# Last 64 rows of three weight matrices on partitions 0 to 63, in 8-row transfers, used as K=64 matmuls

## The chip, the cores and the metric

One core of one Trainium2 chip runs the whole kernel. The metric is the device time of one execution in microseconds (us), the median over the runs.

## The reference

A decode step for one token: attention with a K/V cache of 8 heads x 65,536 positions x 256 (bfloat16), a gated feed-forward block, and a scalar gate between the two. Cut to what matters:

```python
x: [1, 1, 448]                    # D = 448 = 3 * 128 + 64
q    = x @ wq                     # wq [448, 4096], 16 query heads of 256
a    = softmax(q k^T / 16) v @ wo # k_cache, v_cache: 268 MB each
gate = x @ W_gate;  up = x @ W_up # [448, 1792] each
b    = (gate * (gate > 0) * up) @ W_down
out  = g * a + (1 - g) * b        # g = sigmoid(sum(x * gate_w))
```

Almost all bytes are the cache. The change touches only `wq`, `W_gate` and `W_up`, and of those only the last 64 of 448 rows (the *remainder*), which do not fill 128 partitions.

## The kernel before

Three SBUF buffers of 8 MB form a ring. The cache is streamed in 8 MB tiles (32 for K, 31 for V, and a last V tile in pieces), all issued by one queue (SP). `ring[2]` first holds `wq`, `W_gate`, `W_up` and then `W_down`. So the *third K tile* can only be issued when the matmuls of `W_down` are done.

```python
order = [("wq", 0, 8.7), ("k", 0, TILE), ("gu", 0, 7.7), ("wd", 0, 3.8)]   # then k1, k2, k3, v0, k4, ...
slot, held, freed = {}, {2: ["gu", "dn"]}, {}     # ring[2] is free after gate/up and W_down
# ...
# remainder: 64 rows cut in two halves, 128 partitions, row r in partitions 2r and 2r+1
l_["wqh"] = dma("sp", ..., wqh, A_wq[NR3:D, :].rearrange("r (t n) -> (r t) n", t=2))
dma("sp", ..., wfh[i_], W[NR3:D, :].rearrange("r (t f) -> (r t) f", t=2))
# ...
def f_gu(e):                                      # gate/up, 28 output columns of M_ps
    for ft in range(FT):
        for which in range(2):
            c = which * 14 + ft
            for kt in range(R3):                  # three matmuls with K=128
                e.matmul(GU_ps[:, c:c + 1], wf3[which][:, kt * F + ft:(kt + 1) * F:FT], xT[:, kt:kt + 1],
                         start=(kt == 0), stop=False, skip_group_check=True)
            for half in range(2):                 # two matmuls, 64 output partitions each
                ins = e.matmul(GU_ps[64 * half:64 * half + 64, c:c + 1], wfh[which][:, ft:F // 2:FT],
                               xT[:, R3 + half:R3 + half + 1], start=False, stop=True, skip_group_check=True)
# ... cut: score, softmax, P x V, output projection
```

The program of PE (the matmul engine; DVE below is the vector engine) runs in this order at the start: q (with `wq`), gate/up, the scores of the first K tile, `W_down`.

## Time and profile before

| | before |
|---|---|
| time, median of 3 runs | 1287.91 us (1287.82 to 1288.36) |
| time of the profiled execution, one more | 1287.13 us |
| bytes loaded | 549 MB, 428 GB/s over the span |
| DMA, PE, DVE | 99% of 16 DMA engines, 33%, 49% |
| steady distance of two tiles | 19.36 us |

The execution that the profile shows was 0.7 us faster than the fastest of the timed ones.

The page of the kernel before, cut to its span, the busy times of the compute engines (us, share, x instructions) and two DMA queues (packets, MB, share of 16 engines):

```profile
span 1285.3 us, 9821 instructions
...
PE 430.0 (33%) x4554; PEld 161.6 (13%) x4554; DVE 633.8 (49%) x421; ACT 61.4 (5%) x115; POOL 4.1 (0%) x21
...
q1 hardware_dynamic: 12754, 549.03, 99.1%
q8 instruction: 35, 0.57, 0.2%
```

The load queue q1 keeps the 16 DMA engines busy for practically the whole span; no compute engine comes near. The second queue, q8, loads instructions: 35 packets.

The DMA issues of the kernel before (what is loaded, the issuing queue, count, KB each, us from issue to landing):

```profile
ring<-in_A_wq_dram SPq DMA_DIRECT2D x1, 3072.0 KB, 10.1
...
ring<-in_A_wq_dram SPq DMA_DIRECT2D x1, 512.0 KB, 10.9
ring<-in_A_k_cache_dram SPq DMA_DIRECT2D x32, 51.6
ring<-in_A_v_cache_dram SPq DMA_DIRECT2D x31, 36.7
...
ring<-in_B_W_up_dram SPq DMA_DIRECT2D x1, 224.0 KB, 35.2
```

A tile needs 19.36 us of transfer but lands 37 to 52 us after its issue: two or more tiles are always queued. An engine that finishes its part of one tile goes on with the next at once (within some 4 ns in the median, from the packet records). There is one place at the start where this is not so. The timeline of the kernel before, 36 to 66 us (start, duration, engine, line, operation):

```profile
39.34 0.31 PE L418 MATMUL M_ps<-xT,ring 128*128 128x1 bf16 x3 [16.49 <-DMA ring<-in_B_W_up_dram]
39.58 0.28 PE L421 MATMUL M_ps<-xT,ring 128*64 128x1 bf16 x2
39.79 0.34 PE L418 MATMUL M_ps<-xT,ring 128*128 128x1 bf16 x3
...
52.79 5.05 PE L345 MATMUL ST<-ring,xm 128*16 128x512 bf16 x64
57.64 2.81 PE L434 MATMUL A_ps<-ring,hT 128*1 128x448 bf16 x14
60.48 0.80 SPq L442 DMA_DIRECT2D ring<-in_A_k_cache_dram  x2
```

Gate/up starts when `W_up` has landed and repeats a group of three and two matmuls every 0.48 us, up to 52.8 us; the first scores and `W_down` follow; at 60.48 the queue issues the next two K tiles. That the queue really waited for `W_down` is told by the waits of the issuing queue (who waited for whom: total us, times, longest):

```profile
SPq L507 <- PE ST L345: 951.9, 30, 36.5
...
SPq L442 <- PE A_ps L434: 37.6, 1, 37.6
```

The first line is an ordinary wait for a ring buffer with a full queue behind it. The second is the one that matters. In the packet records of the trace the second K tile runs out on the 16 engines between 61.0 and 62.8 us, 0.5 to 2.3 us after that issue, and the median engine then needs 20.94 us for the third K tile instead of 19.35: about 1.6 us lost. I call this the *restart loss*.

Transfer times count here from the first instruction of each trace, as the timelines do. The prediction counts its transfer times from another zero, 0.24 us earlier in this trace: its "61.2 to 63.0" is the 61.0 to 62.8 above.

Last, where the end comes from. These are the 16 landings (each 0.3 to 0.5 us after the end of a packet, so taken as one per DMA engine; sorted, us after the first) of one transfer each in the trace of the kernel before:

```
second K tile     first 61.43   0 .08 .12 .15 .16 .18 .32 .33 .46 .52 .53 .58 .74 1.49 1.76 1.78
third K tile      first 82.28   spread up to 2.52
last whole V tile first 1243.42 0 .17 .26 .35 .37 .49 .84 | 4.14 6.11 6.19 6.20 6.28 6.38 6.44 | 8.38 8.61
```

The engines drift apart over the run. Seven stay together, one ends 4 us behind, six about 6 us, two 8.4 to 8.6 us behind. The last one sets the end: in 15 of the 18 traces of this case the execution ends 34.7 to 35.5 us after that last landing.

### The profile page before, as it was taken

The numbers are of one execution on the slowest core, as the hardware profiler recorded it, in microseconds if no ns is written. First come the engines' busy times: TensorE is split into PE (matmuls) and PEld (weight loads), VectorE is DVE, ScalarE is ACT, GpSimd is POOL, SyncE is SP. The second block draws the span as 40 slices with busy tenths as digits, with TensorE's granted clock in tenths as the row PEclk, the third lists the DMA queues.
The fourth block names the chain that finished last, engine by engine and source line by source line (L and its number), as shares of the span: only waits on it lengthen the run. The fifth ranks groups of instructions, "written<-read, shape, count | busy, mean of one in ns | idle before, by whom it ended". The sixth has DMA issues, their size and how long they took to land.

```text
span 1285.3 us, 9821 instructions
## 1 busy us (share of the span) xinstructions
PE 430.0 (33%) x4554; PEld 161.6 (13%) x4554; DVE 633.8 (49%) x421; ACT 61.4 (5%) x115; POOL 4.1 (0%) x21
## 2 busy tenths in 40 slices
PE   3624322334123432224331333331323323233236
PEld 2401110111001110001110111110101101011111
DVE  2588633465433655434555443555434556335600
ACT  0000000000000000000000000000000000000000
POOL 1000000000000000000000000000000000000000
PEclk8656666656566565666655666665666656666576
DMA  9999999999999999999999999999999999999997
GB/s 399 421 425 447 423 430 441 431 429 435 437 424 437 431 439 428 429 433 441 425 431 449 423 429 439 433 423 443 435 423 441 435 425 433 437 431 437 430 401 304
DMA packets 12798, 549.65 MB, mean 428 GB/s; under 512 B 1235, under 2 KB 3542, under 8 KB 3670
## 3 DMA queue, kind: packets, MB, share of 16 engines
q1 hardware_dynamic: 12754, 549.03, 99.1%
q8 instruction: 35, 0.57, 0.2%
q14 instruction: 5, 0.04, 0.0%
q10 hardware_dynamic: 4, 0.00, 0.0%
HBM read 549.03 MB, written 0.00 MB: 427 GB/s over the span
## 4 chain that ended last, share of the span: by engine, by line
DVE 34%; DMA 32%; another core or an unknown queue 16%; PE 15%; SPq 1%; ACT 1%; issue 1%; ACTq 0%
DVE ring L333 30%; DMA ring<-in_A_k_cache_dram 27%; PE ST L345 7%; PE O L367 6%; DMA ring<-in_B_W_up_dram 3%; DMA ring<-in_A_wo_dram 2%; DVE P_sb L470 1%; SPq L511 1%; DVE nmb L448 1%; PE PT L475 1%; PE M_ps L418 1%; PE M_ps L421 0%; ACT ptp L484 0%; DVE o_sb L378 0%
## 5 line engine op out<-in xcount | busy, mean ns | idle before, releaser
L333 DVE STREAM_TRANSPOSE ring<-ring 128x2048 uint32<-128x2048 uint32 x256 | 565.4, 2275 | 412.7 <-DMA ring<-in_A_k_cache_dram 412.7
L345 PE MATMUL ST<-ring,xm 128*16 128x512 bf16 x2048 | 224.2, 613 | 758.4 <-DVE ring L333 758.4
L345 PEld LDWEIGHTS ST<-ring,xm 128*16 128x16 bf16 x2048 | 61.4, 121 | 907.0 <-DVE ring L333 798.4
L367 PE MATMUL O<-ring,ptp 128*4 128x512 bf16 x2048 | 147.8, 451 | 31.2 <-DMA ring<-in_A_v_cache_dram 27.1
L450 ACT ACTIVATE P_sb<-ST,nmb 128x512 bf16<-128x512 f32 x32 | 45.5, 1420 | 1115.1 <-DVE nmb L448 1115.1
L448 DVE TENSOR_REDUCE nmb<-ST 128x1 f32<-128x512 f32 x32 | 22.1, 689 | 110.4 <-PE ST L345 110.4
L367 PEld LDWEIGHTS O<-ring,ptp 128*4 128x4 bf16 x2048 | 54.0, 98 | 124.4 <-issue 56.0
L378 DVE CAST o_sb<-O 128x512 bf16<-128x512 f32 x8 | 5.5, 692 | 80.8 <-PE O L367 80.8
L470 DVE TENSOR_TENSOR P_sb<-P_sb,hs 128x1024 bf16<-128x1024 bf16 x16 | 18.9, 1222 | 8.5 <-ACT hs L464 8.5
L475 PE MATMUL PT<-identb,P_sb 128*128 128x128 bf16 x128 | 16.6, 311 | 15.5 <-DVE P_sb L470 14.7
L418 PE MATMUL M_ps<-xT,ring 128*128 128x1 bf16 x84 | 9.5, 205 | 16.5 <-DMA ring<-in_B_W_up_dram 16.5
L475 PEld LDWEIGHTS PT<-identb,P_sb 128*128 128x128 bf16 x128 | 12.3, 141 | 18.3 <-DVE P_sb L470 18.3
L484 ACT COPY ptp<-PT 128x256 bf16<-128x256 bf16 x32 | 10.3, 375 | 23.0 <-PE PT L475 23.0
L305 PE MATMUL M_ps<-ring,P_sb 128*128 128x256 bf16 x64 | 9.9, 334 | 3.1 <-DMA ring<-in_A_wq_dram 3.1
L418 PEld LDWEIGHTS M_ps<-xT,ring 128*128 128x128 bf16 x84 | 7.2, 152 | 17.1 <-issue 16.7
L450 ACT ACTIVATION_READ_ACCUMULATOR P_sb<-ST,nmb 128x1 f32 x32 | 8.6, 268 | 0.0
L534 PE MATMUL A_ps<-ring,attnT 128*1 128x448 bf16 x32 | 8.0, 406 | 1.2 <-DMA ring<-in_A_wo_dram 1.1
L305 PEld LDWEIGHTS M_ps<-ring,P_sb 128*128 128x128 bf16 x64 | 7.6, 120 | 5.1 <-issue 3.1
L421 PE MATMUL M_ps<-xT,ring 128*64 128x1 bf16 x56 | 7.8, 276 | 0.0
L401 DVE STREAM_TRANSPOSE ptp<-P_sb 128x128 uint32<-128x128 uint32 x1 | 0.3, 311 | 13.2 <-ACT P_sb L400 13.2
L460 PE MATMUL M_ps<-identf,hs 128*2 128x128 f32 x8 | 2.5, 308 | 10.0 <-DVE hs L458 10.0
L421 PEld LDWEIGHTS M_ps<-xT,ring 128*64 128x64 bf16 x56 | 5.4, 191 | 0.4
(71 smaller groups left out, 60.7 us busy)
## 6 DMA issues: line engine op xcount, KB each, us to landing
ring<-in_A_v_cache_dram SPq DMA_DIRECT2D x1, 4096.0 KB, 30.7
ring<-in_A_wq_dram SPq DMA_DIRECT2D x1, 3072.0 KB, 10.1
ring<-in_A_wo_dram SPq DMA_DIRECT2D x1, 2688.0 KB, 31.2
ring<-in_A_v_cache_dram SPq DMA_DIRECT2D x1, 2048.0 KB, 22.9
ring<-in_A_v_cache_dram SPq DMA_DIRECT2D x2, 1024.0 KB, 25.5
ring<-in_B_W_down_dram SPq DMA_DIRECT2D x1, 1568.0 KB, 20.8
ring<-in_B_W_gate_dram SPq DMA_DIRECT2D x1, 1344.0 KB, 32.5
ring<-in_B_W_up_dram SPq DMA_DIRECT2D x1, 1344.0 KB, 35.1
```

Of the source, the lines that this page charges most:

```text
L305: ins = e.matmul(QN_ps, xw3[:, k_, 31 - j:159 - j], rhs, start=(j == 0 and kt == 0), stop=(j == J - 1 and kt == R3))
L333: return lambda e: e.transpose(v, v)
L345: ins = e.matmul(bank[32 * w:32 * w + 16, :], xm[:, x0:x0 + 16], ktv[sl][:, u0:u0 + 16, c, :, r_], start=(b == 0 and c == 0 and r_ == 0), ...
L367: ins = e.matmul(OP[h % 2][32 * g:32 * g + 4, :], ptp[h % 2][:, col:col + 13:4], ring[sl][:, k * 512:(k + 1) * 512], start=(a == 0 and k < ...
L418: e.matmul(GU_ps[:, c:c + 1], wf3[which][:, kt * F + ft:(kt + 1) * F:FT], xT[:, kt:kt + 1], start=(kt == 0), stop=False, skip_group_check= ...
L421: ins = e.matmul(GU_ps[64 * half:64 * half + 64, c:c + 1], wfh[which][:, ft:F // 2:FT], xT[:, R3 + half:R3 + half + 1], start=False, stop= ...
L448: smax[n] = op("dv", tk + 22, lambda e, n=n, NM=NM, t_=t_: e.tensor_reduce(NM[:, t_:t_ + 1], ST[n % 2][:], AX.X, ALU.max, negate=True), [q ...
L450: aexp[n] = op("ac", tk + 23, lambda e, n=n, t_=t_, NM=NM, RS=RS: e.activation(P_sb[:, t_:2048:4], ST[n % 2][:], ACTF.Exp, bias=NM[:, t_:t ...
L470: rsc = op("dv", tt, lambda e, X=X, pb=pb: e.tensor_tensor(pb, pb, X[:, 12:16].unsqueeze(1).to_broadcast([128, 256, 4]), ALU.mult), [h7, a ...
L475: ins = e.transpose(PT[rd][:, s * 128:(s + 1) * 128], P_sb[:, (rd * 8 + s) * 128:(rd * 8 + s + 1) * 128], identb[:, :])
L484: ins = e.copy(dst, src)
L511: dep = dma("sp", t, "vp%d" % i, lambda e, sl=sl, n=n, lo=lo, hi=hi: e.dma_start(ring[sl][:, lo * 256:hi * 256], v_src(n)[:, lo * 256:hi * ...
```

## The change

Intent: put each 64-row remainder on 64 partitions in one piece, so that one matmul with K=64 replaces two half-column matmuls per output column of gate/up (28 instead of 56). Each remainder is loaded in 8 transfers of 8 rows, with a partition step of 4. The core of the diff, with the bookkeeping of `x` (a fourth column of 64 values instead of two interleaved ones) cut:

```diff
-        wqh = ring[2][:, R3 * NQ:R3 * NQ + NQ // 2]
+        wqh = ring[2][:, R3 * NQ:(R3 + 1) * NQ]
 ...
+        def rows64(sem, t, dst, W):
+            for i in range(8):
+                b0 = i % 4 + 32 * (i // 4)
+                d_ = dma("sp", t + 0.0001 * i, sem, lambda e, b0=b0: e.dma_start(
+                    dst[b0:b0 + 29:4, :], W[NR3 + b0:NR3 + b0 + 29:4, :]))
+            return d_
 ...
-                l_["wqh"] = dma("sp", ..., A_wq[NR3:D, :].rearrange("r (t n) -> (r t) n", t=2)))
+                l_["wqh"] = rows64("wqh", t + 0.01, wqh, A_wq)
 ...            (f_q: 48 matmuls with K=128, then 16 with K=64; 64 in all, as before)
                 def f_gu(e):
                     for ft in range(FT):
                         for which in range(2):
                             c = which * 14 + ft
                             for kt in range(R3):
                                 e.matmul(GU_ps[:, c:c + 1], ..., xT[:, kt:kt + 1],
-                                         start=(kt == 0), stop=False, skip_group_check=True)
-                            for half in range(2):
-                                ins = e.matmul(GU_ps[64 * half:64 * half + 64, c:c + 1], ...)
+                                         start=(c == 0 and kt == 0), stop=False, skip_group_check=True)
+                    for ft in range(FT):
+                        for which in range(2):
+                            c = which * 14 + ft
+                            ins = e.matmul(GU_ps[:, c:c + 1], wfh[which][0:KR, ft:F:FT], xT[0:KR, R3:NX],
+                                           start=False, stop=(ft == FT - 1), skip_group_check=True)
```

The order changes too: all K=128 matmuls first, then all K=64 ones.

More of the change, by code (lines that the diff above doesn't have):

```diff
@@ L117, in bass_gated_mix__gqa_block_cached__glu_gated_reglu__decode_kernel @@
     NR3 = R3 * 128
-    NX = R3 + 2
+    NX = R3 + 1
     FT = F // 128
@@ L123, in bass_gated_mix__gqa_block_cached__glu_gated_reglu__decode_kernel @@
     assert DH == 256 and NQ == J * DH and J <= 32 and NTH * TK == S and NTH == 4
-    assert D - NR3 == 64 and FT * 128 == F and FT <= 14 and FT % 2 == 0 and D <= 448 and H >= 3
+    KR = D - NR3
+    assert KR == 64 and FT * 128 == F and FT <= 14 and FT % 2 == 0 and D <= 448 and H >= 3
     es = ExitStack()
@@ L162, in bass_gated_mix__gqa_block_cached__glu_gated_reglu__decode_kernel @@
         gw_row = ptp[1][0:1, 0:D]
-        xeo = ptp[1][0:1, 448:704]
         qrep = ptp[1][:, 704:960]
@@ L167, in bass_gated_mix__gqa_block_cached__glu_gated_reglu__decode_kernel @@
         wq3 = ring[2][:, 0:R3 * NQ]
-        wqh = ring[2][:, R3 * NQ:R3 * NQ + NQ // 2]
-        WB = R3 * NQ + NQ // 2
+        wqh = ring[2][:, R3 * NQ:(R3 + 1) * NQ]
+        WB = (R3 + 1) * NQ
         wf3 = [ring[2][:, WB + i * R3 * F:WB + (i + 1) * R3 * F] for i in range(2)]
         WB += 2 * R3 * F
-        wfh = [ring[2][:, WB + i * (F // 2):WB + (i + 1) * (F // 2)] for i in range(2)]
-        assert WB + F <= U * DH
+        wfh = [ring[2][:, WB + i * F:WB + (i + 1) * F] for i in range(2)]
+        assert WB + 2 * F <= U * DH
         wd_sb = ring[2][:, 0:FT * D].rearrange("p (ft d) -> p ft d", ft=FT)
@@ L237, in bass_gated_mix__gqa_block_cached__glu_gated_reglu__decode_kernel @@
         c_o1 = op("dv", -0.2, lambda e: e.memset(one_t[:], 1.0))
-        c_xe = op("dv", -0.1, lambda e: e.memset(xeo, 0.0))
         c_xw = op("dv", 0, lambda e: e.memset(xw, 0.0))
@@ L278, in bass_gated_mix__gqa_block_cached__glu_gated_reglu__decode_kernel @@
         z7 = mop("dv", 1.7, lambda e: e.tensor_copy(gb[:], GB_ps), [z6])
-        def f_xeo(e):
-            e.tensor_copy(xeo[0:1, 0:128:2], x_row[0:1, NR3:D])
-            return e.tensor_copy(xeo[0:1, 129:256:2], x_row[0:1, NR3:D])
-        x0_ = op("dv", 0.5, f_xeo, [d_x, c_xe])
         def f_xT(e):
-            for kt in range(NX):
-                src = x_row[0:1, kt:NR3:R3] if kt < R3 else xeo[0:1, (kt - R3) * 128:(kt - R3 + 1) * 128]
-                ins = e.matmul(XT_ps[:, kt:kt + 1], src, one_t[0:1, 0:1], start=True, stop=True)
-            return ins
@@ L291, in bass_gated_mix__gqa_block_cached__glu_gated_reglu__decode_kernel @@
-        x1_ = mop("pe", 0.6, f_xT, [d_x, x0_, c_o1])
-        x2_ = mop("dv", 0.7, lambda e: e.tensor_copy(xT[:], XT_ps), [x1_])
-        xw3 = xw.rearrange("p (kt c) -> p kt c", kt=NX)
-        q0 = op("dv", 0.9, lambda e: e.tensor_copy(
-            xw3[:, :, 31:160:32], xT[:].unsqueeze(2).to_broadcast([128, NX, 5])[:, :, 0:5]), [x2_, c_xw])
+            for kt in range(R3):
+                e.matmul(XT_ps[:, kt:kt + 1], x_row[0:1, kt:NR3:R3], one_t[0:1, 0:1], start=True, stop=True)
+            return e.matmul(XT_ps[0:KR, R3:NX], x_row[0:1, NR3:D], one_t[0:1, 0:1], start=True, stop=True)
@@ new lines, in bass_gated_mix__gqa_block_cached__glu_gated_reglu__decode_kernel, with f_xT2, f_xw @@
+        x1_ = mop("pe", 0.6, f_xT, [d_x, c_o1])
+        def f_xT2(e):
+            e.tensor_copy(xT[:, 0:R3], XT_ps[:, 0:R3])
+            return e.tensor_copy(xT[0:KR, R3:NX], XT_ps[0:KR, R3:NX])
+        x2_ = mop("dv", 0.7, f_xT2, [x1_])
+        xw3 = xw.rearrange("p (kt c) -> p kt c", kt=NX)
+        def f_xw(e):
+            e.tensor_copy(xw3[:, 0:R3, 31:160:32], xT[:, 0:R3].unsqueeze(2).to_broadcast([128, R3, 5])[:, :, 0:5])
+            return e.tensor_copy(xw3[0:KR, R3:NX, 31:160:32],
+                                 xT[0:KR, R3:NX].unsqueeze(2).to_broadcast([KR, 1, 5])[:, :, 0:5])
@@ L299, in f_q @@
+        q0 = op("dv", 0.9, f_xw, [x2_, c_xw])
         def f_q(e):
             for j in range(J):
-                half, jj = divmod(j, J // 2)
-                for kt in range(R3 + 1):
-                    k_, rhs = (kt, wq3[:, kt * NQ + j * 256:kt * NQ + (j + 1) * 256]) if kt < R3 else \
-                        (R3 + half, wqh[:, jj * 256:(jj + 1) * 256])
-                    ins = e.matmul(QN_ps, xw3[:, k_, 31 - j:159 - j], rhs,
-                                   start=(j == 0 and kt == 0), stop=(j == J - 1 and kt == R3))
+                for kt in range(R3):
+                    e.matmul(QN_ps, xw3[:, kt, 31 - j:159 - j], wq3[:, kt * NQ + j * 256:kt * NQ + (j + 1) * 256],
+                             start=(j == 0 and kt == 0), stop=False, skip_group_check=True)
+            for j in range(J):
+                ins = e.matmul(QN_ps, xw3[0:KR, R3, 31 - j:159 - j], wqh[0:KR, j * 256:(j + 1) * 256],
+                               start=False, stop=(j == J - 1), skip_group_check=True)
@@ L396, in bass_gated_mix__gqa_block_cached__glu_gated_reglu__decode_kernel @@
                 l_["wq"] = dma("sp", t, "wq", lambda e: e.dma_start(wq3, A_wq[0:NR3, :].rearrange("(p k) n -> p (k n)", k=R3)))
-                l_["wqh"] = dma("sp", t + 0.01, "wqh", lambda e: e.dma_start(wqh, A_wq[NR3:D, :].rearrange("r (t n) -> (r t) n", t=2)))
+                l_["wqh"] = rows64("wqh", t + 0.01, wqh, A_wq)
                 tq = tL["wq", 0]
@@ L409, in bass_gated_mix__gqa_block_cached__glu_gated_reglu__decode_kernel @@
                         wf3[i_], W[0:NR3, :].rearrange("(p k) f -> p (k f)", k=R3))))
-                    a1.append(dma("sp", t + 0.01 * i_ + 0.005, "wfh%d" % i_, lambda e, W=W, i_=i_: e.dma_start(
-                        wfh[i_], W[NR3:D, :].rearrange("r (t f) -> (r t) f", t=2))))
+                    a1.append(rows64("wfh%d" % i_, t + 0.01 * i_ + 0.005, wfh[i_], W))
                 def f_gu(e):
@@ L418, in f_gu @@
                                 e.matmul(GU_ps[:, c:c + 1], wf3[which][:, kt * F + ft:(kt + 1) * F:FT], xT[:, kt:kt + 1],
-                                         start=(kt == 0), stop=False, skip_group_check=True)
-                            for half in range(2):
-                                ins = e.matmul(GU_ps[64 * half:64 * half + 64, c:c + 1], wfh[which][:, ft:F // 2:FT],
-                                               xT[:, R3 + half:R3 + half + 1], start=False, stop=True, skip_group_check=True)
+                                         start=(c == 0 and kt == 0), stop=False, skip_group_check=True)
[4 more added lines that the diff above has]
+                                           start=False, stop=(ft == FT - 1), skip_group_check=True)
                     return ins
```

## The prediction

> **What bounds the kernel now.** The 16 DMA engines. The queue table has the load queue in 99.1% of 16 engines' span: 549 MB in 1285.3 us, 428 GB/s. In the trace's packet records a 65,536-byte packet takes 2.42 us (27.1 GB/s) nearly always, 8,064 times; an 8 MB tile takes 8 x 2.42 = 19.36 us, the steady distance of the landings. Cache transfers land 37 to 52 us after issue (DMA table), about two tiles, so the queue is normally never empty.
>
> The change touches the first 65 us (timeline): wq's matmuls run 12.1 to 22.0; gate/up's 39.3 to 52.8, released by W_up's last rows; the first scores to 57.8; W_down's to 60.5, which frees the ring buffer for the third K tile, issued at 60.9. The tile before it runs out at 61.2 to 63.0, so this issue is just too late: each engine's first two packets take about 3.2 and 2.9 us instead of 2.42, a loss of 1 to 1.5 us. Only here does PE time touch the DMA stream.
>
> **What the change does.**
> 1. Bytes stay the same (960 KB in three remainders). Before, each spreads over 128 partitions; now a transfer has 8 rows. [...] So all 24 transfers should use the same 8 engines, one row each; this trace cannot show it. Those carry 60 KB more, the others 60 KB less. By packet times: before, 8 x 0.159 + 16 x 0.0765 = 2.50 us each; after, 8 x 0.311 + 16 x about 0.14 (estimate between 1,792 and 4,096 bytes) = 4.75 us on eight engines, 0 on the others: +2.3 and -2.5 us.
> 2. 21 more issues at about 0.45 us: SP finishes by about 16 us, before the engines need it. No cost.
> 3. Gate/up: 56 matmuls of 64 columns become 28 of K=64; a group falls from 0.48 to about 0.36 us, the total from 13.5 to about 10.1 us. It starts 2.3 us later (41.6) and ends about 51.7 instead of 52.8. wq keeps 64 matmuls, started 1.2 us later; hidden.
> 4. The third K issue comes about 1 us earlier.
>
> **On the critical path.** For the eight loaded engines: +2.3 us, minus the 1.5 us restart loss, which vanishes because they still have work: about +0.7. The others run dry early and restart about 1.2 us sooner than before. At the end one transfer's landings spread over 6.5 us: laggards set the end. If one of the three slowest is among the loaded eight (likely), the end moves +0.7; if not, about -1.
>
> **Predicted: 1288.4 us, range 1286.6 to 1290.4.** Faster by over 2%: 0.01; within 2%: 0.98; slower by over 2%: 0.01.
>
> **What would show it.** 64 packets of 8,192 bytes and 128 of 3,584, on eight engines only; wq's remainder landing at 13.5 instead of 12.3; gate/up as 112 matmuls in about 10 us; third K issue near 60 us; the second K tile's landings split in two groups 4 to 5 us apart; tile distance still 19.36 us.
>
> **What would make it wrong.** A fixed cost per small transfer [...]; rows landing on fewer engines; the two groups' split not hidden by queue depth; instruction fetches moving the laggards.

Two passages are cut: a rule for how many engines an 8-row transfer uses, which no trace shows, and a figure for a fixed cost per small transfer, which none shows either. That all 24 transfers use the same eight engines was an assumption; the trace of the changed kernel, below, bears it out (8 packets of 8,192 bytes and 16 of 3,584 on each of eight).

## More of the kernel before

The durations of the two kinds of gate/up matmul, from the view of their lines (ns: min/median/max; first and last start in us):

```profile
L418 PE MATMUL M_ps<-xT,ring x84: 193/198/223, 39.3 to 52.4; 128*128 128x1 bf16 x84
...
L421 PE MATMUL M_ps<-xT,ring x56: 275/276/277, 39.6 to 52.6; 128*64 128x1 bf16 x56
```

## The result, and the profile after

| | before | after |
|---|---|---|
| median of 4 runs | 1288.13 us | 1286.15 us |
| runs | 1287.91, 1287.82, 1288.36, 1288.35 | 1288.04, 1285.96, 1286.34, 1285.85 |

The ratio is 0.9988 with a 95% interval of 0.9971 to 1.0005: within 2%, and not clear of 1. Ratios here are the mean time of one kernel's fast runs over the mean of the other's of the same rounds, so not quite the ratio of the medians. All these runs are fast (granted clock 0.619 to 0.625 in the four of the changed kernel, 0.628 in the profiled execution of the kernel before). The profiled run of the changed kernel is the slowest of its four, 1288.04 us; its span is even longer than that of the profile before, which was a fast execution of its kernel (1287.13 us). Any reading of this one trace as "the" changed kernel would mislead.

The page after, same lines as before:

```profile
span 1286.2 us, 9784 instructions
...
PE 428.1 (33%) x4525; PEld 156.2 (12%) x4525; DVE 633.2 (49%) x420; ACT 61.2 (5%) x115; POOL 4.1 (0%) x21
...
q1 hardware_dynamic: 12706, 549.03, 99.0%
q8 instruction: 35, 0.57, 0.2%
```

Nothing has changed at this level: same bytes, same share, the same 35 instruction packets. The DMA issues after:

```profile
ring<-in_A_wq_dram SPq DMA_DIRECT2D x1, 3072.0 KB, 10.2
...
ring<-in_A_wq_dram SPq DMA_DIRECT2D x8, 64.0 KB
ring<-in_A_k_cache_dram SPq DMA_DIRECT2D x32, 51.9
ring<-in_A_v_cache_dram SPq DMA_DIRECT2D x31, 36.7
ring<-in_B_W_gate_dram SPq DMA_DIRECT2D x8, 28.0 KB
ring<-in_B_W_up_dram SPq DMA_DIRECT2D x8, 28.0 KB
```

The timeline after, 36 to 66 us:

```profile
42.31 5.17 PE L427 MATMUL M_ps<-xT,ring 128*128 128x1 bf16 x84 [17.85 <-DMA ring<-in_B_W_up_dram]
...
47.41 1.84 PE L432 MATMUL M_ps<-xT,ring 64*128 64x1 bf16 x28
49.18 5.88 PE L345 MATMUL ST<-ring,xm 128*16 128x512 bf16 x64
...
54.88 2.81 PE L445 MATMUL A_ps<-ring,hT 128*1 128x448 bf16 x14
...
57.72 0.80 SPq L453 DMA_DIRECT2D ring<-in_A_k_cache_dram  x2
```

Gate/up starts 3.0 us later, because the last remainder lands later (42.06 us instead of 39.06), but takes 6.9 us (42.3 to 49.2) instead of 13.5. The third K tile is issued at 57.72 instead of 60.48. The wait of the issuing queue shrinks accordingly:

```profile
SPq L453 <- PE A_ps L445: 33.2, 1, 33.2
```

The two kinds of gate/up matmul after; the K=64 ones are as short as the full ones:

```profile
L427 PE MATMUL M_ps<-xT,ring x84: 194/198/198, 42.3 to 47.3; 128*128 128x1 bf16 x84
...
L432 PE MATMUL M_ps<-xT,ring x28: 194/195/217, 47.4 to 49.1; 64*128 64x1 bf16 x28
```

The sorted landings of the same transfers as above, after:

```
second K tile     first 59.17   0 .01 .09 .22 .31 .56 .68 1.43 | 4.70 4.75 4.77 4.88 4.89 5.45 5.68 6.89
third K tile      first 79.66   0 ... .40 (eight)              | 3.54 3.61 3.64 3.74 3.75 4.29 4.53 5.74
last whole V tile first 1240.70 0 .36 3.64 3.74 4.14 4.25 4.26 6.31 6.32 6.39 6.43 6.49 6.52 6.59 | 10.17 12.22
```

Eight engines now run about 4.8 us behind the other eight after the remainders. Here the trace can be read engine by engine. A packet of one engine starts within a few nanoseconds of the end of the one before (4 ns in the median from 75 to 1205 us), so the packet records can be chained into 16 engines; the chain is checked by the order of packet sizes that each engine must carry. The 64 packets of 8,192 bytes and 128 of 3,584 bytes of the remainders fall into exactly eight chains, 8 and 16 in each, and never more than eight of a size run at once. I call these engines *loaded* and the others *light*. The method can mistake two engines for each other where they start at the same moment, which happens at the restart and late in the run; I use sorted landings, which need no chaining, wherever they suffice.

The chains also show what the drift is. When one of the 35 packets of 16,384 bytes on q8 passes, one engine pauses: its next cache packet starts about 1.0 us late (0.9 to 1.1) and mostly takes 2.9 to 3.0 us instead of 2.42. From 75 to 1205 us eight engines take three or four such hits each, the other eight none. In the trace before, the engines without a hit reach the end of the third-last whole tile at a median of 1204.6 us, those with hits at 1210.6: (1210.6 - 1204.6) / 4 = 1.5 us per fetch.

The eight engines take the fetches in turn: chained once more over 14 traces, 251 of 299 pairs of successive hits on one engine are eight fetches apart, and the rest may be mistaken engines. So the engines of the first and the second fetch (at 44 and 56 us here, near 48 and 55 after the change) also get the 33rd and the 34th of the 35, and carry five by 1230 us where the others have four.

| third-last whole tile, us | before | after, six traces |
|---|---|---|
| engines without late fetches | 1204.6 | light 1200.9 to 1201.7, loaded 1205.5 to 1205.8 |
| engines with three or four late fetches | 1210.6 | light 1206.9 to 1207.9, loaded 1211.3 to 1212.5 |
| last engine | 1212.6 | 1211.5 to 1213.5, always loaded |

(Medians of a group, in us from the first instruction; the groups are those of the chained packets, the times those of the landings less 0.43 us, which is about the time from a packet's end to its landing. The six traces are the one above, and those of `after_again`, `look1` to `look3` and `after_b` below.)

### The profile page after: what moved, and what is told of

The parts are those of the page before. It is cut to its first block, busy times and chain, and to the rows that moved or that the text cites. A ratio compares the mean times of both kernels' runs of the same rounds, so it can differ in the third digit from the quotient of the medians.

```text
span 1286.2 us, 9784 instructions
## 1 busy us (share of the span) xinstructions
PE 428.1 (33%) x4525; PEld 156.2 (12%) x4525; DVE 633.2 (49%) x420; ACT 61.2 (5%) x115; POOL 4.1 (0%) x21
## 4 chain that ended last, share of the span: by engine, by line
DVE 34%; DMA 31%; another core or an unknown queue 16%; PE 15%; SPq 2%; ACT 1%; issue 1%; ACTq 0%
DVE ring L333 30%; DMA ring<-in_A_k_cache_dram 27%; PE ST L345 7%; PE O L376 6%; DMA ring<-in_A_wo_dram 2%; DMA ring<-in_B_W_up_dram 2%; DVE P_sb L481 1%; SPq L356 1%; SPq L522 1%; DVE nmb L459 1%; PE PT L486 1%; PE M_ps L427 0%; ACT ptp L495 0%; DVE o_sb L387 0%
## 5 line engine op out<-in xcount | busy, mean ns | idle before, releaser
L486 PEld LDWEIGHTS PT<-identb,P_sb 128*128 128x128 bf16 x128 | 12.3, 140 | 18.3 <-DVE P_sb L481 18.3
L427 PE MATMUL M_ps<-xT,ring 128*128 128x1 bf16 x84 | 5.2, 198 | 17.9 <-DMA ring<-in_B_W_up_dram 17.9
L473 PE MATMUL M_ps<-mx,nselT 2*128 2x1 f32 x16 | 4.2, 332 | 3.0 <-DVE mx L472 3.0
```

The lines of the kernel that those rows point to most:

```text
L486: ins = e.transpose(PT[rd][:, s * 128:(s + 1) * 128], P_sb[:, (rd * 8 + s) * 128:(rd * 8 + s + 1) * 128], identb[:, :])
```

## The experiments

The theories, as the expectations name them. **A**: the slowest of the 16 engines sets the end; its time is the bytes it carries, plus the restart loss, plus about 1.5 us per instruction fetch. **A2** is the form that A took later: the last engine is a loaded one with four late fetches, plus an early one in some runs. Rivals: **B**, a uniform gain, and idle PE time is free; **C**, the transfers' split is what gains, not PE time; **D**, the drift of the engines has nothing to do with instruction fetches; **E**, the gain is the shorter gate/up stage alone.

Each call ran its kernels on one chip; the chips of different calls differ. Medians are of fast runs; "before" is the kernel before in the same rounds.

### after_again: the change once more

No edit; five rounds.

> The changed kernel unedited, for its spread. Theory A (the slowest of 16 DMA engines sets the end; engines lose about 1.5 us per 16 KB instruction fetch that they carry, and which engines carry a fifth fetch changes from run to run): two values, about 1285.8 to 1286.4 where a loaded engine carries four fetches, about 1288.0 where it carries five; before stays at 1287.8 to 1288.4 in all runs, because there some engine always has five. Rival B (a uniform gain): one value near 1286, with 1288.04 a stray.

Measured: 1286.41 us (1285.98 to 1286.79), before 1287.92 (1286.28 to 1288.28, 9 runs), ratio 0.9992 (0.9979 to 1.0004). One value, no run at 1288, while before showed two runs of nine at 1286.3 and 1286.6. So theory A as worded is not confirmed: the kernel before is not fixed at 1288 either. The trace, however, ends its last whole V tile at 1251.18 us where the slow run has 1252.92.

### one64: one transfer of 64 rows

```diff
-            for i in range(8):
-                b0 = i % 4 + 32 * (i // 4)
-                d_ = dma(... dst[b0:b0 + 29:4, :], W[NR3 + b0:NR3 + b0 + 29:4, :]))
+            return dma("sp", t, sem, lambda e: e.dma_start(dst[0:KR, :], W[NR3:D, :]))
```

> Each remainder as one transfer of 64 rows to partitions 0 to 63, matmuls as in the change. Theory A: all 16 engines carry the same bytes, no split, and the gate/up stage stays short, so the third K issue comes in time and the restart loss of about 1.5 us is gone: about 1286.7, one value only. If 64 partitions are reached at half the rate, the remainders take 2.2 us more on every engine and it is about 1288.8; the landings of wq's remainder (1.3 us after wq in the kernel before) show which. Theory C (the split over eight engines is what gains): no gain, 1288.1 or more.

Measured: 1289.24 us (1288.81 to 1289.79), before 1287.92, ratio 1.0014 (1.0002 to 1.0027): the second case of the expectation, 0.4 us beyond it. The DMA issues of this kernel:

```profile
ring<-in_A_wq_dram SPq DMA_DIRECT2D x1, 3072.0 KB, 11.3
...
ring<-in_A_wq_dram SPq DMA_DIRECT2D x1, 512.0 KB, 13.1
```

The last landings of wq and of its remainder are 2.31 us apart (12.02 and 14.33), against 1.25 us before (10.78 and 12.03). The 64 packets of 8,192 bytes take 0.62 us each (median) where those of the change, on eight engines at a time, take 0.31. Sixteen engines with 8,192 bytes each in 0.62 us are 211 GB/s, no more than the eight engines of the change move in their 0.31 us, and half of the 428 over the span: the half rate of the expectation. All 16 engines now lose the time together: the engines without fetches reach the mark of the table above at 1207.6 us. There was no restart loss (third K tile in 19.35 us), so this is the cost of the slower packets, net of that. The runs show the doubled packet time, not its reason. The obvious simpler form of the change is slower than the kernel before, by 1.3 us.

### grouped and grouped_ok: the order of the matmuls alone

```diff
                             for kt in range(R3):
                                 e.matmul(GU_ps[:, c:c + 1], ...,
-                                         start=(kt == 0), stop=False, ...)
-                            for half in range(2):
-                                ins = e.matmul(...)
+                                         start=(c == 0 and kt == 0), stop=False, ...)   # grouped: start=(kt == 0)
+                    for half in range(2):
+                        for ft in range(FT):
+                            for which in range(2):
+                                c = which * 14 + ft
+                                ins = e.matmul(...)
```

> The kernel before with the gate/up matmuls in grouped order alone (84 with K=128, then 56 of 64 columns); all transfers as before. Theory A: gate/up takes about 9 to 10 us instead of 13.5, the third K issue comes near 57 us instead of 60.9, before the tile ahead of it runs out at 61.2, and the restart loss is gone: about 1286.7. Theory C: PE time does not count, 1288.1.

`grouped` kept a start flag for every output column and gave a wrong result, relative error 0.079. `grouped_ok`, which differs in the start flags alone (only the first matmul sets one), is correct. So a start for every column is wrong in the new order, while the kernel before sets the same flags in the old one; why, no run shows. The time of the wrong one is valid: 1286.45 us (1285.79 to 1287.16), before 1287.92.

> The kernel before with only the order and the start flags of the gate/up matmuls changed, now with a correct result [...]. Theory A: as the wrong one of the first batch, 1286.4, so the whole gain of the change comes from the shorter gate/up stage, none from the transfers. Theory C (the transfers' part is needed): 1287.9.

Measured: 1286.10 us (1285.72 to 1287.18), before 1287.81, ratio 0.9988 (0.9974 to 1.0001). Its timeline, 36 to 70 us:

```profile
39.65 5.17 PE L418 MATMUL M_ps<-xT,ring 128*128 128x1 bf16 x84 [17.18 <-DMA ring<-in_B_W_up_dram]
44.76 6.25 PE L424 MATMUL M_ps<-xT,ring 128*64 128x1 bf16 x56
...
58.97 0.80 SPq L445 DMA_DIRECT2D ring<-in_A_k_cache_dram  x2
```

The same 140 matmuls take 11.3 us (39.65 to 50.94) instead of 13.5. In the kernel before, 28 groups alternate three matmuls of 128x128 weights with two of 128x64, and not mixing them gives 2.2 us; what it is in the alternation that costs this time, no run here shows. The 56 half matmuls still cost 0.11 us each. The issue comes 1.5 us earlier than before, less than `grouped` was expected to bring (near 57 us); the median engine needs 19.49 us for the third K tile instead of 20.94 (the mean 19.71 instead of 20.87: some still lose about 2), and the engines without fetches reach the mark at 1203.6 us, 1.1 us ahead of before. With all transfers as they were, this gains as much as the whole change. Its traced execution took 1286.79 us though its last whole V tile ended 1.9 us ahead of before (1250.10): the next transfer landed 8.4 us later instead of 7.0, which fits the fetch at 1254.4 us on the last engine.

### gu_twice: a late third K tile

The gate/up matmuls of the change, all 112, run twice.

> The changed kernel with its gate/up matmuls run twice (same result), so that the third K issue is late: near 64.5 us. Theory A: every engine waits for that issue, the split of the engines is gone after it, and the time grows by how much later than 60.9 us the issue comes: about 1291.5 to 1292. Rival B: 7 us of PE work at 33% load are hidden, about 1286.

Measured: 1289.64 us (1289.06 to 1289.93), before 1287.92, ratio 1.0016 (1.0004 to 1.0029). The timeline shows the issue:

```profile
64.55 0.80 SPq L453 DMA_DIRECT2D ring<-in_A_k_cache_dram  x2
```

Every engine waits, and the third K tile lands on all 16 within 0.9 us (85.71 to 86.60): the split is wiped out. Direction and place are as theory A said, but the size is missed: +1.7 us instead of +4. The engines without fetches are indeed 3.7 us behind before. The last engine is not: before, the last ones had already lost 2 us by then (third K tile at 84.81), here nobody has (86.60), a difference of 1.79. That was the clue to what follows: *the last engine of the kernel before is not an ordinary one*. It carries an instruction fetch before 65 us as well as four later ones.

### fetch_more and fetch_less: the instruction fetches

`fetch_more` adds 2048 one-column matmuls, overwritten by the real ones, to the kernel before; `fetch_less` leaves out 896 P x V matmuls (relative error 0.46). Its output is wrong, which doesn't matter for the time.

```diff
+                for i in range(64 if b == 0 else 0):                       # fetch_more, in f_qk
+                    w = i % 4
+                    e.matmul(bank[32 * w:32 * w + 16, 0:1], xm[:, 8:24], ktv[sl][:, w * 16, 0, 0:1, 0], start=True, stop=True, ...)
+                    if 4 <= k < U // 2 - 4 and k % 8 >= 4:                 # fetch_less, in f_pv
+                        continue
```

> The kernel before with 2048 one-column matmuls more in the score stage (their result is overwritten), 64 per K tile, some 4 us of PE per 19.4 us tile pair at 33% PE load. Theory A: the program grows by 4096 instructions, the trace shows about 16 more 16 KB instruction packets (51 instead of 35), each engine that carries them gets two more, each costs it about 1.5 us: about 1291 (1290 to 1292). Rival D (lag of some engines has nothing to do with instruction fetches): PE has room, 1287.9.

> The kernel before with 896 of the 2048 P x V matmuls left out (wrong result on purpose), which takes some 1792 instructions away, all transfers unchanged. Theory A: about 7 instruction packets fewer (28 instead of 35), one fewer on most of the engines that carry them: about 1286.4. Rival D: PE is not on the path, 1287.9.

Measured: `fetch_more` 1290.10 us (1289.43 to 1290.71), ratio 1.0018 (1.0005 to 1.0030); `fetch_less` 1285.98 us (1285.65 to 1286.06), ratio 0.9985 (0.9973 to 0.9998); before 1287.81 for both. The instruction queue of `fetch_more`, then of `fetch_less`:

```profile
q8 instruction: 51, 0.84, 0.3%
```

```profile
q8 instruction: 28, 0.46, 0.1%
```

51 and 28 packets, exactly as expected (4096 instructions more are 16 packets more, 1792 fewer are 7 fewer: 256 to a packet), and both times move the way theory A says. The times alone also hold the changed PE work; the engines tell the two apart. At the mark the eight fetch-carrying engines lie 4.9, 6.0 and 9.1 us (medians) behind the other eight with 24, 31 and 45 late packets on the queue (`fetch_less`, before, `fetch_more`), that is 3, 3.9 and 5.6 each: 1.5 to 1.6 us per fetch in all three. Rival D is out. Two caveats. The dummies of `fetch_more` also delay the third K issue (62.31 us), which puts even the engines without fetches 1.0 us behind; in the trace of `fetch_less` these are 0.6 us ahead. And the last engine's distance to the first, in the last whole V tile, grows only from 8.61 to 10.04 us in `fetch_more`: with the late issue the third K tile lands on all 16 within 0.85 us, so whatever the early fetches had cost was wiped out, as in `gu_twice`. In `fetch_less` the same distance is 7.58 us.

### gu_split: a smaller split

wq's remainder as before (128 partitions); the remainders of gate/up in 8-row transfers with K=64, grouped.

> Gate/up's remainders as in the change (8-row transfers, K=64, grouped), wq's remainder as in the kernel before. Theory A: the eight loaded engines carry 28 KB more instead of 60 KB, so they lie about 1.2 us ahead of where the change has them, and the others 1.2 us behind: the eight loaded ones still set the end, about 1285.5 (1285.0 to 1286.2) in most runs. Rival (the split costs nothing): as grouped, 1286.4.

Measured: 1284.75 us (1284.54 to 1286.63), before 1287.81, ratio 0.9980 (0.9968 to 0.9993). Correct. The third K tile is issued earliest of all:

```profile
55.94 0.81 SPq L455 DMA_DIRECT2D ring<-in_A_k_cache_dram  x2
```

Loaded engines without late fetches are at 1204.4 us, light ones at 1202.1, and no engine has a restart loss (19.35 us on both sides). The last loaded engine (1210.3) and the last light one (1209.7, with an early fetch) are nearly level. The gain is at the top of what was expected.

### pad and pad_b: the transfers' part with a later third K tile

```diff
                 def f_gu(e):
+                    for c in range(13):
+                        for kt in range(R3):
+                            e.matmul(GU_ps[:, c:c + 1], ...)      # 39 matmuls done once more ahead
```

> The changed kernel with the first 39 gate/up matmuls run once more ahead of the rest (same result), so that the gate/up stage ends about 2.4 us later and the third K issue comes near 61 us, where the kernel before has it: the transfers' part of the change without the shorter stage. Theory A: the eight loaded engines run out of the second K tile only at 63.6 to 66, so an issue at 61 is still in time for them, and the others lose slack that they have: as the change, 1286.4 (1285.8 to 1287.0), or a little more if an engine of the light half had an early instruction fetch. Theory E (after the order experiment: the gain is the shorter stage alone): no gain left, 1288 or more, up to 1290 with the 2.3 us of the loaded engines.

Measured: 1287.14 us (1286.12 to 1287.47), before 1287.17 (1286.40 to 1289.23), ratio 0.9992 (0.9978 to 1.0006). The issue comes at:

```profile
60.03 0.80 SPq L456 DMA_DIRECT2D ring<-in_A_k_cache_dram  x2
```

The strong form of theory E (1290) is out. The loaded engines took 19.5 us for the third K tile and so lost almost nothing, the light ones 23.0. But the median missed theory A's range by 0.14 us and equals that of before, which on this chip was itself 0.7 us lower; between A and the weak form of E this run does not decide.

### look1, look2, look3: more traces of the change

No edit, one execution each, on the chip of `pad`.

> The changed kernel again, for its trace. Theory A2: the last engine of all is a loaded one that carries four late instruction fetches; the run is near 1286.2 if the two or three early fetches (before 65 us) fell on light engines, near 1288 if one fell on a loaded engine.

> The changed kernel once more, for its trace. Theory A2 as for the look before: near 1286.2 if the early instruction fetches fell on light engines, near 1288 if one fell on a loaded engine that carries late ones too.

> The changed kernel once more, for its trace. Theory A2 as for the look before: near 1286.2 if the early instruction fetches fell on light engines, near 1288 if one fell on a loaded engine that carries late ones too.

Measured: 1287.02, 1287.60 and 1287.41 us; before 1287.17 on this chip. Between the two values expected, for a reason that the six traces of the change show. The two instruction fetches at about 48 and 55 us fall on different engines from run to run:

```
trace        fetch near 48 us   fetch near 55 us   last landing, last whole V tile   time of the run
after_b      light              light              1250.86                            1285.74
after_again  light              light              1251.18                            1286.22
look1        light              loaded             1252.36                            1287.02
look3        light              loaded             1252.07                            1287.41
look2        light              loaded             1252.12                            1287.60
first trace  loaded             light              1252.92                            1288.04
```

In all six, exactly two engines land more than 10 us behind the first in the last whole V tile (the next are at 8.2 us or less), and the chains say that these two are loaded ones with late fetches. An early fetch on a light engine is nearly absorbed, since that engine waits for the third K tile anyway; on a loaded engine it makes that one the last and the end 0.9 to 2.1 us later. (In the three looks the step shows only after the mark, when this engine takes its fifth fetch near 1229 us: its distance to the first engine goes from 10.5 to 10.8 us to 11.5 to 12.3 in one tile.) The six runs come from different chips, three of unknown state; the order of the times is a pattern of six, not a test.

### after_b, grouped_b, gu_split_b, pad_b: all on one chip

> The changed kernel, unedited, on one chip with the three that follow. Theory A2 (last engine = a loaded one with four late instruction fetches, plus 1 to 2 us if an early fetch hit it): 0.5 to 1.5 us under before, its runs spread over 2 us.

> The order alone. Theory A2: every engine is 1.1 to 1.5 us earlier than in before, early fetches cost what they cost there: 1.2 to 1.7 us under before, equal to the change within 0.5 us.

> Split of gate/up's remainders alone (28 KB more on eight engines) with the short stage. Theory A2: about 1.2 us under the change, 2 to 3 us under before. Rival (a split is worth nothing beside the order): equal to the order alone.

> The changed kernel with its gate/up stage padded by 2.4 us. Theory A2: equal to the change within 0.7 us, under before by 0.5 to 1.5 us, since the loaded engines still have work when the third K issue comes. Theory E: before or above it.

| | median (range) | mean | ratio to before (95%) |
|---|---|---|---|
| before, 9 runs | 1287.35 (1286.36 to 1288.88) | 1287.42 | |
| after_b | 1286.46 (1285.74 to 1287.50) | 1286.61 | 0.9995 (0.9983 to 1.0008) |
| grouped_b | 1286.23 (1285.77 to 1286.48) | 1286.14 | 0.9992 (0.9979 to 1.0004) |
| pad_b | 1286.45 (1285.58 to 1287.26) | 1286.51 | 0.9994 (0.9982 to 1.0007) |
| gu_split_b | 1285.94 (1284.75 to 1286.52) | 1285.71 | 0.9987 (0.9974 to 1.0001) |

All four lie 0.9 to 1.4 us under before in the median, none of them clear of 1 at 95%. The padded change equals the change (means 0.1 us apart), as theory A2 says and theory E does not; since neither is clear of before, this speaks against E and does not rule it out. The order alone equals the change within 0.5 us. `gu_split` is again the fastest, but 0.9 us under the change in the mean, less than the 1.2 expected, and its lead over the order alone (0.4 us) is inside the spread; on the other chip it was 1.1 us in the mean. Its mean is under that of before on both chips (clear of noise on the first alone) and under that of the change on the one where both ran; the step over the order alone is not settled.

## Why the prediction was right or wrong

**The limit, right.** The DMA engines bound the kernel; bytes, rate and tile distance did not move.

**The split over eight engines, right.** The prediction assumed that all 8-row transfers use the same eight engines, which no trace had shown then; the packet chains after the change show exactly eight, with 8 and 16 packets each and 0.309 and 0.140 us per packet (costed at 0.311 and about 0.14). The two halves were to be 4.8 us apart (2.3 + 2.5); the second K tile's landings show 4.7 us between their first members. No fixed cost per small transfer appeared.

**The issue cost, right in effect.** SP took 0.67 to 0.68 us per small issue, more than the 0.45 estimated, and was still ahead of the engines.

**Gate/up, right in direction, mis-sized.** 10.1 us was predicted, 6.9 measured. I read 0.48 us per mixed group and subtracted one of two half matmuls. But the K=128 matmuls cost only 5.17 / 84 = 0.062 us each when they are not mixed, so part of what I kept was the mixing itself. `grouped_ok` isolates it: 2.2 us from the order, and a further 4.4 us (6.25 to 1.84) from 28 K=64 matmuls in place of 56 half ones. So the third K issue came 2.8 us earlier (60.48 to 57.72) instead of 1, and the light engines came out 2.9 to 3.7 us ahead of before instead of 1.2.

**The step that failed: "If one of the three slowest is among the loaded eight (likely), the end moves +0.7; if not, about -1."** The condition held: in all six traces the two last engines are loaded ones. The size for a loaded engine was roughly right when compared with an engine of the same kind: without late fetches they are 1.1 us behind before (1205.7, the median of the six, against 1204.6), where I had 0.7. But the conclusion for the end does not follow, because the last engine of the traced kernel before is 2 us behind the other fetch carriers (1212.6 against 1210.6): an early instruction fetch, before 65 us, fell on it. In the changed kernel the last engine is a loaded one that carries four fetches, or five where it also has an early one. Without it the last whole V tile ends at 1250.86 and 1251.18 us, 0.8 to 1.2 us sooner than before (1252.03); with it, 0.0 to 0.9 us later, on both sides of my +0.7. So the step took for granted that the last engine carries the same fetches after the change as before. The runs of the first measurement were mostly of the first sort if their times tell, for only the one of 1288.04 us was traced, and the median fell 0.45 us under my range. I had named "instruction fetches moving the laggards" as a risk and given it no number; its number is 1.5 us per fetch, as large as the restart loss. Whether a run of the change gains or loses against the traced execution of before depends on where the early fetches fall, which is no part of the change: so far the sign of the result is luck.

**Where the gain comes from.** As far as the traces show it, the common part is the restart loss of about 1.6 us. The order alone takes it away by an earlier issue; the split takes it away for the loaded engines by leaving them work at the restart, even with a late issue (`pad`); `gu_twice` brings it back for all. The two ways do not add up. The split then costs the loaded engines 2.3 us, which the whole change pays and `gu_split` pays only in part.

**Open.** Why 6 of the 8 fetch-carrying engines are light in every trace of the change, and what decides which engine carries an early fetch, no run tells. Nor is it shown what sets apart the runs of before near 1286.4 or near 1288: the only trace of before is of an execution of 1287.13 us. The engines account for the distance of the change's runs to that one; the other 1.0 us up to the first measurement's median of 1288.13 has no trace. The change itself is not clear of 1 at 95% in any of its three timed comparisons (0.9988, 0.9992, 0.9995), though all three point the same way.

## What to carry to other kernels

When 16 DMA engines are the limit and the queue is deep, they need not end together (8.6 us apart in the last whole V tile before, 12.2 after): ask which single engine ends last and what it carried, before adding a term to "the" DMA time. Where a buffer is freed just before the queue runs dry, a few microseconds of an otherwise idle engine count up to the size of that gap: an issue 1.5 us earlier put the engines 1.1 us ahead (`grouped_ok`), one 4.1 us later put them 3.7 us behind (`gu_twice`), though its end only 1.7. Try the order of the same instructions first: here it gained as much as new transfers, new layout and half the small matmuls together.

How far ahead of running dry the next large transfer must be issued, these runs show for this kernel alone. With the issue 0.5 us before the first engine ended the second K tile, the 16 engines lost 1.5 us in the mean (before); at 1.0 us the eight light engines of the change lost 0.9; at 2.1 us the loss was 0.4 (`grouped_ok`, 58.97 to 61.06); at 3.8 us it was nothing (`gu_split`).
